# A forward FFT without butterflies until its last units, with memory handed over tile by tile, in a kernel of two joined problems

## The chip, the cores and the metric

The kernel runs on one core of one Trainium2 chip. The metric is the device time of the program in microseconds (us) on that core. The kernel before took 780.77 us, the median of three runs (777.03, 780.77 and 781.84).

TensorE (PE) multiplies matrices, VectorE (DVE), ScalarE (ACT) and GpSimd (POOL) work element by element, and SyncE (SP) issues transfers. "PEld" is the loading of PE's weights, beside PE. A transfer (DMA) is issued from a queue of SP or POOL and lands later.

## The reference, cut to what matters

Two independent problems are computed and joined along the last axis.

```python
# A: 32 heads of 18, 2048 rows in 4 segments of 512
q, k, v = x @ wq, x @ wk, x @ wv            # 2048 x 576, split into heads
M, z = 0, 0
for s in range(4):
    logits = qs @ ks.T * 18**-0.5 + mask    # causal, 512 x 512 a head
    a_dot = softmax(logits) @ vs
    a_mem = (phi(qs) @ M) / (phi(qs) @ z + 1e-6)
    o = g * a_mem + (1 - g) * a_dot         # g = sigmoid(beta)
    M, z = M + phi(ks).T @ vs, z + phi(ks).sum(rows)
a = concat(o) @ wo                          # phi(t) = t + 1 if t > 0 else exp(t)
# B: 2048 x 576
b = irfft2(rfft2(x) * (w_r + 1j * w_i), s=(2048, 576))
return concatenate([a, b], axis=-1)
```

## The kernel before, in words

float32 accuracy comes from splitting an operand into a high and a low part (a rounded copy, and what the copy leaves) and multiplying three times. The order of the instructions is written out by hand: the code runs under a manual schedule, so an engine executes its instructions in the order in which the Python code emits them. The framework adds the semaphore waits. Loops advance generators: a `yield` is a place at which another piece of work may be put in between, so moving a `yield` moves instructions in their engine's order.

There are four stages, named here by the classes `FFT` and `ATT`.

**Forward transform** (`FFT.forward`, L109 to L196, from 0 to 76.7 us). Problem B's 2048 rows are cut by 16 and transformed along both axes by matmuls, in a pipeline of 20 iterations u for 16 units. `prep` (two units ahead) forms sums and differences on DVE (`eo`, L125), their high part on ACT (`eh`, L127) and their low part on DVE (`el`, L131, and `eh`, L132). `f1` is 14 matmuls (L142). `ev0` copies the result to X on ACT (L146), and `ev1` subtracts on DVE for its low part (L149). `c1` is 12 matmuls (L162), three iterations after f1. `evz` copies c1's result from PSUM to Z on ACT (L153), four iterations after f1. The weights of the projections are loaded and split in between (`wqkl`, L391, on DVE), and the first tiles of x.

What remains of B's transform across the 16 units are radix-4 butterflies on Z: `bf` (L206; each yields after each of ten DVE instructions), `tws` (twiddles, ACT and DVE), the product with w (in `middle`) and, for the inverse, `last`. These are steps of one DVE instruction each, held in a queue, `Pace`; `take(f)` adds f to an account and runs a step for each whole unit of it. There are 266 steps in all. In the forward transform `take(1)` is called ahead of the end of prep for u below 14 (the queue has work from u = 7), and `take(2)` at the end of an iteration for u from 14.

**Projections** (`ATT.projections`, L517 on, 76.7 to 285 us). x @ wq, wk, wv in 4 segments of 13 units (`pj` and `pjv`, L445; `pm`, L502, for M and z). They run butterfly steps at an even rate that leaves `pace.left-8` as the total to be done here.

**Inverse** (`FFT.inverse`, 285 to 378 us). `ysplit` splits Z into Y (ACT, L280; the low part on POOL, L281). `i2` is 18 matmuls (L296), whose result is copied and split to T (ACT L322 and L328, DVE L324 and L329), `i3` 14 matmuls (L307), and `out` (DVE L314, L315) stores `yb` (L316). Each unit takes one butterfly step; where `ysplit(u+2)` needs a block of four that isn't finished, it runs all steps that are still missing at once (`while s.done<b and s.pace.one()`), which can be at u = 2, 6 and 10. A prologue of attention is put between: on SP's queue the loads of Qs and Ks (`stack_dmas`, L600), then the mask and beta (L840), and on PE the row maxima of the first ten heads.

**Attention** (`ATT.attention`, to the end). 133 steps t, one head each: `s1` of head t+10 gives the row maxima (L616 scores on PE, L620 and L626 on DVE; the causal block is added by a matmul of `tri` with `idb`, L625), `s2` (L660 to L670) the scores again and their exponentials on ACT, `pv` (L687) the product with v. When four heads have their maxima, `mpath` takes them to a row of Qs: `mg` on DVE and ACT, `mh` on POOL (L642 high, L643 low), a transpose on PE (`mt`, L646), a copy, and a transfer. In the loop `mpath(k+2)` is begun at hh = 1, runs its second part (mh) at hh = 2, the transpose at hh = 3, the copy right behind. `affine_select` (L672) clears what is above the diagonal, on POOL. Behind this, `run_bg` advances a list of later work: late setup (`ob`, the load of wo), `combine(g)`, which scales by reciprocals `rr` (L780 is its matmul) and adds on POOL (`am`, L786; `ol`, L776), `mem1` and `oproj`. A `lane` computes the reciprocals: for g = 1 it waits 2 more steps before loading `ux`, loading `rr` and appending combine to the list.

Memory comes from pools, which are opened and closed by stage. When a pool is closed and another takes its place, the first tile of the new one waits for everything that used the old one. So tiles of `pp` (projections) wait for all of `pf` (forward), and the tiles of attention (`tp2`, `ps`) for all of the inverse's, its stores included.

The lines on which the prediction's steps turn are these.

```python
            if t in (3,7): m=s.mpath(t//4); next(m); next(m)
...
            if hh in (2,3) and m is not None: steps(m,1)
            if hh==1 and k+2<32: m=s.mpath(k+2); next(m)
```

Of the kernel before, what the change touches and what calls it, by code (L numbers as in the profile page):

```python
# [102 lines left out]
class FFT:  # L103
# [4 lines left out]
    def forward(s,xp,cp,pp,wl,xs,consts):  # L108

        nc,io=s.nc,s.io; v=nc.vector  # L110
        xin={}; cw={}; C={}; eh={}; el={}; F={}; X={}
        def load(u):
            xin[u]=xp.tile([128,2,3,128],F32,name="xin",bufs=3)
            nc.sync.dma_start(xin[u],io["xb"][u])
        def loadc(u):
            a,b=BORD[u]
            cw[u]=cp.tile([128,2,384],F32R,name="cfw",bufs=4)
            nc.gpsimd.dma_start(cw[u],io["cfw"][4*a+b].rearrange("p (h m) -> p h m",h=2))
        def prep(u,halves=False):

            x=xin.pop(u)
            eo=xp.tile([128,2,3,128],F32,name="eo",bufs=2)
            h=xp.tile([128,2,3,128],F32R,name="eh",bufs=3)
            for r,op in enumerate((OP.add,OP.subtract)):
                v.tensor_tensor(eo[:,r],x[:,0],x[:,1],op=op)  # L125
                if halves: nc.scalar.copy(h[:,r],eo[:,r])
            if not halves: nc.scalar.copy(h,eo)  # L127
            yield
            l=xp.tile([128,2,2,128],F32R,name="el",bufs=3)
            for w in (slice(0,1),slice(1,2)) if halves else (slice(0,2),):  # L130
                v.tensor_tensor(l[:,w],eo[:,w,:2],h[:,w,:2].bitcast(F32),op=OP.subtract)  # L131
                v.tensor_tensor(h[64:97,w,2],eo[64:97,w,2],h[64:97,w,2].bitcast(F32),op=OP.subtract)  # L132
            eh[u],el[u]=h,l
            yield
        def f1(u):
            p=pp.tile([128,2,512],F32,name="f1",tag="f1")
            h,l=eh.pop(u),el.pop(u)
            for r in range(2):
                L=[(h[:,r,0],tab[:,0,r,0]),(h[:,r,1],tab[:,0,r,1]),(h[:,r,0],tab[:,1,r,0]),(h[:,r,1],tab[:,1,r,1]),
                   (l[:,r,0],tab[:,0,r,0]),(l[:,r,1],tab[:,0,r,1]),(h[:99,r,2],tab2[:99,r])]  # L140
                for n,(x,t) in enumerate(L):
                    nc.tensor.matmul(p[:,r,:FP],x,t,start=n==0,stop=n==6)  # L142
            F[u]=p
        def ev0(u):
            x=xp.tile([128,2,FP],F32R,name="X0",bufs=3); X[u]=[x]
            nc.scalar.copy(x,F[u][:,:,:FP])  # L146
        def ev1(u):
            x=xp.tile([128,2,FP],F32R,name="X1",bufs=3)
            v.tensor_tensor(x,F.pop(u)[:,:,:FP],X[u][0].bitcast(F32),op=OP.subtract)  # L149
            X[u].append(x)  # L150
        def evz(u):
            a,b=BORD[u]
            for r,p in enumerate(C.pop(u)): nc.scalar.copy(s.Z[:,b,a,r],p[:,:FP])  # L153
        def c1(u):
            a,b=BORD[u]; x=X.pop(u); cc=cw.pop(u)
            for r in range(2):
                p=pp.tile([128,512],F32,name="c1",tag="c1")
                n=0
                for (i,hl) in ((0,0),(0,1),(1,0)):
                    for q in range(2):  # L160
                        k=(0 if q==0 else 2) if r==0 else (1 if q==0 else 0)
                        nc.tensor.matmul(p[:,:FP],cc[:,hl,k*128:(k+1)*128],x[i][:,q],start=n==0,stop=n==5)  # L162
                        n+=1
                C.setdefault(u,[]).append(p)
        load(0)
        tab=cp.tile([128,2,2,2,FP],F32R,name="ftab",bufs=1)
        tab2=cp.tile([128,2,FP],F32R,name="ftab2",bufs=1)
        nc.gpsimd.dma_start(tab[:,0],io["ftab"][:,:4*FP].rearrange("p (r c f) -> p r c f",r=2,c=2))
        late=consts()
        nc.gpsimd.dma_start(tab[:,1],io["ftab"][:,4*FP:].rearrange("p (r c f) -> p r c f",r=2,c=2))  # L170
        nc.gpsimd.dma_start(tab2,io["ftab2"].rearrange("p (r f) -> p r f",r=2))
        load(1); load(2); late()
        for u in range(2): loadc(u)
        p=[prep(u,True) for u in range(2)]
        for i in range(2):
            for x in p: next(x)
        load(3)
        s.pace=Pace(61+165+40)
        for u in range(20):
            p=prep(u+2) if u+2<16 else iter(())  # L180
            if 0<u<17: ev0(u-1)
            if 3<u: evz(u-4)
            if u%4==3 and u>6: s.pace.add(s.stage1((u-7)//4))
            next(p,None)
            if 0<u<17: ev1(u-1)
            if u<14: s.pace.take(1)
            next(p,None)
            if u<16: f1(u)
            if u+4<16: load(u+4)
            elif u<18: next(xs,None)  # L190
            if 2<u<19: c1(u-3)
            if 0<u<15: loadc(u+1)
            if 1<u: next(wl,None)
            if u>13: s.pace.take(2)
        for _ in wl: pass
        for _ in xs: pass  # L196
    def bf(s,x,y,inv):
# [173 lines left out]
class ATT:  # L371
# [147 lines left out]
    def projections(s,xp,tp,pp,wv,pace,hook):  # L519

        live=[]
        s.nid=wv.tile([128,128],BF,name="nid"); s.nc.scalar.activation(s.nid,s.ident,AF.Copy,scale=-1.0)
        lw=s.load_w("wv",576,wv,xp,288,"xl",4)
        def advance():
            for l in list(live):
                try: next(l)
                except StopIteration: live.remove(l)
        tot=pace.left-8
        for g in range(4):
            if g<3: xq=[s.xprep(g+1,t,(xp,s.x0)[g%2],xp,[128,512],"xst",2) for t in range(5)]  # L530
            for i in range(13):
                u=s.qk_unit(g,i,tp,pp) if i<9 else s.v_unit(g,i-9,tp,pp)
                if i==4 and g<3: s.pk=tp.tile([128,4,576],F32,name="pk",bufs=1)
                next(u)
                hook(g,i)
                next(lw,None); next(lw,None)
                if g<3 and i in (4,6,8,10,12): next(xq[(i-4)//2])
                if g<3 and i in (1,3,5,7,9): next(xq[(i-1)//2])
                w=tot/(36+16*2.4)*(1.0 if i<9 else 2.4)
                advance()  # L540
                pace.take(w*.4)
                advance()
                next(u)
                pace.take(w*.6)
                live.append(u)
        while live: advance()

    def att_setup(s,cp):
# [1 line left out]
        s.Qs=[cp.tile([128,8,512],BF,name=f"Qs{i}") for i in range(3)]  # L550
        s.Ks=[cp.tile([128,8,512],BF,name=f"Ks{i}") for i in range(4)]
        for i in range(4): nc.gpsimd.dma_start(s.Ks[i][108:110].rearrange("p h c -> p (h c)"),io["neg1"])
        s.mask=cp.tile([128,512],F32,name="mask"); s.tri=cp.tile([128,128],BF,name="tri"); s.idb=cp.tile([128,128],BF,name="idb")
        s.bt,s.gt,s.g1=[cp.tile([128,1],F32,name=n) for n in ("bt","gt","g1")]
        d=lambda n,sh,dt: s.dp.tile(sh,dt,name=n)
        s.uD=[d(f"uD{i}",[576,512],F32) for i in range(4)]
        s.rD=[d(f"rD{i}",[32,512],F32) for i in range(4)]
# [76 lines left out]
    def mpath(s,k):  # L634
# [2 lines left out]
        mx=s.mx.pop(k); mg=s.mg.pop(k)  # L637
        nc.vector.tensor_reduce(out=mg[:,:,2:3],in_=mx[:,:,:3],axis=mybir.AxisListType.X,op=OP.max)
        nc.scalar.copy(mg[:,:,0:1],mx[:,:,3:])
        yield  # L640
        mh=s.sm.tile([128,2,16],BF,name="mh",bufs=1); mg=mg.rearrange("p h i -> p (h i)")
        nc.gpsimd.tensor_copy(mh[:,0],mg)  # L642
        nc.gpsimd.tensor_tensor(mh[:,1],mg,mh[:,0],op=OP.subtract)  # L643
# [190 lines left out]
    def prologue(s):  # L834

        nc,io=s.nc,s.io
        for i,f in enumerate(s.stack_dmas(0,0)+s.stack_dmas(0,1)):
            f()
            if i%2==1: yield
        nc.sync.dma_start(s.mask,io["mask"]); nc.sync.dma_start(s.bt,io["beta"])  # L840
        s.load_v(0)
        q=s.stack_dmas(1,0)+s.stack_dmas(1,1)+s.stack_dmas(2,1)+[lambda: s.load_v(1)]
        for i in range(2): yield
        s.masks()
        i=0
        for t in range(10):
            for _ in s.s1(t):
                if q and i%3<2: q.pop(0)()
                i+=1
                yield  # L850
            if t in (3,7): m=s.mpath(t//4); next(m); next(m)
            if t in (4,8): next(m); next(m,None)
        assert not q
    def homes(s):
# [2 lines left out]
    def attention(s,tp,ps):  # L857
# [6 lines left out]
        m=None  # L864
# [12 lines left out]
        for t in range(133):  # L877
# [8 lines left out]
            if st==10 and g>0:  # L886
                def ln(g=g):
                    r=s.recip(s.rD[g-1],s.rrD[g-1],s.g1,False,"rr")
                    for i in range(6):
                        next(r); yield  # L890
                    for i in range(2 if g==1 else 0): yield
                    for u in range(3): s.ux_load(g-1,u)
                    yield from r
                    bg.append(s.combine(g-1))
# [14 lines left out]
            steps(a,1)  # L909
            if hh==3 and m is not None: steps(m,1)  # L910
            steps(b,1)
            if hh in (2,3) and m is not None: steps(m,1)
            if hh==1 and k+2<32: m=s.mpath(k+2); next(m)
            if t>=8 and t%4==0:
                s.pv_out((t-8)//4)
# [61 lines left out]
class PP:  # L977
    def __init__(s,tc,name,bufs): s.tc,s.nm,s.bufs=tc,name,bufs
    def __enter__(s):
        s.cm=s.tc.tile_pool(name=s.nm,bufs=1,space=PSUM); s.p=s.cm.__enter__(); return s  # L980
    def __exit__(s,*a): return s.cm.__exit__(*a)
    def tile(s,sh,dt,name,tag): return s.p.tile(sh,dt,name=name,tag=tag,bufs=s.bufs[tag])
def arrays(x,wq,wk,wv,wo,beta):
# [2 lines left out]
        wo=host_wo(f(wo)).reshape(126,-1),beta=np.repeat(f(beta),4).reshape(128,1),**atables())  # L986
def emit(nc,tc,io):
    def pool(es,name,bufs=1,**kw):
        return es.enter_context(tc.tile_pool(name=name,bufs=bufs,**kw))
    with ExitStack() as L0:  # L990
        cp=pool(L0,"cp"); dp=pool(L0,"dp",space=bass.MemoryType.DRAM)
        A=ATT(nc,tc,io,cp,dp)
# [62 lines left out]
```

## Time and profile before

| | |
|---|---|
| median of three runs | 780.77 us |
| the profiled execution | 779.13 us |
| its span, first to last instruction | 777.3 us |
| PE busy | 718.0 us, 92% of the span |
| mean granted clock of PE | 0.98 |
| bytes moved | 121.64 MB, 156 GB/s |

In a line of the timeline the first number is the start in us from the span's start, the second the duration, then engine, source line, operation, the tiles written and read with their shape, and the count of instructions in the row; in brackets stands the idle time of the engine just before, and what ended it. In a row of windows stand the stretch, its length, the busy time (and count) of PE, PEld, DVE, ACT and POOL, the granted clock of PE as a share of full speed, the busy share of the DMA engines, and GB/s. In a row of groups stand line, engine, operation, tiles, count, busy time, mean ns of one, and the idle time before them. "SPq" is the issue of a transfer, at the time of its issue. What ended a wait is inferred: where several semaphores were waited for, the last by the profile is named.

### The profile page before, as it was taken

What the parts mean: (1) busy time and instruction counts of PE and PEld (TensorE: products, weight loads), DVE (VectorE), ACT (ScalarE), POOL (GpSimd) and SP (SyncE); (2) the same over time, 40 slices, a digit from 0 to 9 for tenths busy, and PEclk for the clock granted to TensorE, in tenths of its full rate; (3) what the DMA queues carried; (4) which work ended last, traced back from release to release, by engine and by line L of the source; (5) the groups of instructions that cost most, each with busy time, mean ns of one, the idle gap of its engine ahead of it and who ended that gap; (6) DMA issues with size and microseconds to landing.
All of it is one profiled execution on the core that took longest, in us unless ns stands there. A gap on an engine that the chain in (4) does not pass through costs nothing.

```text
span 777.3 us, 14564 instructions
## 1 busy us (share of the span) xinstructions
PE 718.0 (92%) x5007; PEld 498.3 (64%) x5007; DVE 546.2 (70%) x1266; ACT 467.5 (60%) x1012; POOL 212.0 (27%) x405
## 2 busy tenths in 40 slices
PE   4998999999999988499898999799999899998997
PEld 4987779788798788499643444333565335642486
DVE  6999878997898875287686878676566665573133
ACT  3666794774784735144486777676566665666621
POOL 2110000101001136154154333362224731337200
PEclk9999999999999999699999999999999999998999
DMA  9883535552642476667477656755447554340142
GB/s 321 280 245 113 174 129 188 188 187 98 225 157 93 165 251 152 171 195 198 130 157 189 168 133 139 180 148 151 119 112 196 142 152 120 91 125 26 27 142 82
DMA packets 81934, 121.64 MB, mean 156 GB/s; under 512 B 8280, under 2 KB 48742, under 8 KB 81724
## 3 DMA queue, kind: packets, MB, share of 16 engines
q1 hardware_dynamic: 75300, 104.63, 46.7%
q0 software_dynamic: 6560, 16.08, 7.3%
q8 instruction: 40, 0.66, 0.3%
q14 instruction: 34, 0.28, 0.1%
HBM read 81.97 MB, written 38.50 MB: 155 GB/s over the span
## 4 chain that ended last, share of the span: by engine, by line
PE 72%; DMA 8%; DVE 7%; ACT 5%; POOL 3%; issue 3%; SPq 0%; DVEq 0%; ACTq 0%; POOLq 0%
PE pj L445 13%; PE pv L687 9%; PE s L616 9%; PE pjv L445 7%; PE po L801 6%; PE i L307 4%; PE i L296 4%; PE s L660 3%; PE s L664 2%; PE po L830 2%; PE s L669 2%; DVE eo L125 2%; PE s L625 2%; DMA xin<-xb 2%; PE pm L502 2%
## 5 line engine op out<-in xcount | busy, mean ns | idle before, releaser
L620 DVE CUSTOM_DVE_ANT_0 junk<-s,mask 128x512 bf16<-128x512 f32 (+1 forms) x256 | 141.6, 553 | 40.5 <-PE s L616 30.4
L616 PE MATMUL s<-Ks,Qs 108*128 108x384 bf16 (+3 forms) x512 | 141.8, 306 | 15.5 <-DMA mask<-mask 11.3
L626 DVE TENSOR_REDUCE mx<-s 128x4 f32<-128x512 f32 x128 | 88.1, 688 | 58.2 <-PE s L625 53.9
L616 PEld LDWEIGHTS <-Qs 108*128 108x128 bf16 x512 | 50.1, 98 | 101.8 <-issue 88.5
L661 ACT ACTIVATE P<-s 128x512 f32<-128x512 f32 x128 | 76.8, 600 | 45.6 <-PE s L660 35.8
L672 POOL TENSOR_SCALAR_AFFINE_SELECT P<-P 128x512 f32<-128x512 f32 x128 | 76.9, 637 | 82.4 <-ACT P L661 82.3
L687 PE MATMUL pv<-P,vs 128*32 128x512 f32 (+3 forms) x1024 | 97.6, 453 | 1.1 <-issue 0.3
L670 ACT ACTIVATE P<-s 128x256 f32<-128x256 f32 x128 | 49.3, 385 | 50.7 <-PE s L669 50.3
L666 ACT ACTIVATE P<-s 128x512 f32<-128x512 f32 x128 | 76.3, 596 | 0.8 <-PE s L665 0.5
L445 PE MATMUL pj<-xh,wqkh 128*128 128x512 f32 x180 | 71.2, 395 | 0.5 <-ACT Z L153 0.5
L445 PE MATMUL pj<-xh,wqkl 128*128 128x512 f32 x180 | 71.1, 395 | 0.0
L445 PE MATMUL pj<-xl,wqkh 128*128 128x512 f32 x144 | 61.8, 429 | 0.0
L660 PE MATMUL s<-Qs,Ks 110*128 110x512 bf16 x128 | 49.3, 385 | 2.5 <-ACT P L661 1.8
L206 DVE TENSOR_TENSOR Z<-t,t 128x290 f32<-128x290 f32 (+1 forms) x96 | 48.7, 556 | 0.1
L445 PE MATMUL pjv<-wvh,xh 128*128 128x288 f32 x160 | 48.1, 303 | 0.0
L445 PE MATMUL pjv<-wvl,xh 128*128 128x288 f32 x160 | 46.2, 295 | 0.0
L206 DVE TENSOR_TENSOR t<-Z 128x580 f32<-128x580 f32 x64 | 45.7, 756 | 0.0
L625 PE MATMUL s<-tri,idb 128*128 128x128 bf16 x256 | 43.6, 222 | 0.5 <-ACT idb L566 0.5
L492 POOL MEMSET vt<- 128x32 f32 x16 | 2.3, 162 | 150.2 <-PE pm L502 125.2
L296 PE MATMUL i<-civ,Y 128*128 128x256 f32 (+1 forms) x288 | 40.6, 293 | 2.8 <-ACT Y L280 1.0
L664 PE MATMUL s<-Qs,Ks 110*128 110x384 bf16 x128 | 42.3, 331 | 0.0
L142 PE MATMUL f<-ftab,eh 128*128 128x290 f32 (+1 forms) x160 | 31.1, 313 | 10.0 <-DMA ftab<-ftab 10.0
(162 smaller groups left out, 1622.6 us busy)
## 6 DMA issues: line engine op xcount, KB each, us to landing
qkD<-sp SPq DMA_DIRECT2D x36, 384.0 KB
Qs<-qkD SPq DMA_DIRECT2D x96, 144.0 KB
Ks<-qkD SPq DMA_DIRECT2D x96, 144.0 KB
xin<-xb SPq DMA_DIRECT2D x16, 384.0 KB
cfw<-cfw POOLq DMA_DIRECT2D x16, 384.0 KB, 4.4
civ<-civ POOLq DMA_DIRECT2D x16, 384.0 KB, 4.3
vs<-vD SPq DMA_DIRECT2D x16, 330.0 KB
vD<-vt SPq DMA_DIRECT2D x16, 311.0 KB
```

The source lines that it names most:

```text
L206: v.tensor_tensor(o,a,b,op=op)
L296: nc.tensor.matmul(p[:m,k],Y[i][:,q,c*128:c*128+m],cc[:,hl,o:o+256],start=n==0,stop=n==5)
L445: s.nc.tensor.matmul(out,a,b,start=i==0,stop=i==len(L)-1)
L616: nc.tensor.matmul(out,Q[:108,h,128*i:128*i+128],K[:108,h,:128*(i+1)],start=True,stop=True)
L620: nc.vector.tensor_tensor_reduce(out=junk[:,:w],in0=src,in1=s.mask[:,512-w:],scale=1.0,scalar=-3.0e38, op0=OP.add,op1=OP.max,accum_out=s.m ...
L625: nc.tensor.matmul(pa[:,o+w-128:o+w],s.idb,s.tri,start=False,stop=True,skip_group_check=True)
L626: nc.vector.tensor_reduce(out=s.mx[k][:,hh],in_=pa.rearrange("p (b c) -> p b c",c=128),axis=mybir.AxisListType.X,op=OP.max)
L660: nc.tensor.matmul(p0,kk(0),q(0),start=True,stop=True)
L661: nc.scalar.activation(P[0][:,hh],p0,AF.Exp,scale=SC)
L666: nc.scalar.activation(P[1][:,hh],p1,AF.Exp,scale=SC)
L672: sel=lambda x,pat: nc.gpsimd.affine_select(out=x,in_=x,pattern=pat+[[1,128]],compare_op=OP.is_ge,fill=0.0,base=0,channel_multiplier=-1)
L687: nc.tensor.matmul(s.pvt[32*hh:32*hh+32,128*j:],vt[:,j,19*h:19*h+32],mv[0][:,hh,mv[1]],start=jj==0,stop=jj==3,skip_group_check=True)
```

## The change

- In the forward transform `evz(u-4)` is emitted ahead of `ev0(u-1)`, so on ACT the copies to Z stand ahead of the copy to X.
- The butterfly steps of the forward transform, one per iteration below u = 14 and two from there, become one for u = 16 to 19.
- The projections run steps up to 18 from the end (before: 8), which leaves 18 for the inverse.
- The loads of mask and beta move from the prologue, behind twelve loads of Qs and Ks, to `att_setup`, ahead of the first of them.
- In `mpath` the first `yield` goes, so mh follows mg at once; in the prologue one `next(m)` goes, and in the loop the advance at hh = 2.
- The lane of g = 1 waits 3 steps where it waited 2.
- All pools, in SBUF and PSUM, hand memory over tile by tile: a new tile waits for the users of the old tiles whose memory it overlaps, and not for the whole old pool.

```diff
@@ FFT.forward
             p=prep(u+2) if u+2<16 else iter(())
+            if 3<u: evz(u-4)
             if 0<u<17: ev0(u-1)
-            if 3<u: evz(u-4)
             if u%4==3 and u>6: s.pace.add(s.stage1((u-7)//4))
             next(p,None)
             if 0<u<17: ev1(u-1)
-            if u<14: s.pace.take(1)
             next(p,None)
             if u<16: f1(u)
...
             if 1<u: next(wl,None)
-            if u>13: s.pace.take(2)
+            if u>15: s.pace.take(1)
@@ ATT.projections
-        tot=pace.left-8
+        tot=pace.left-18
@@ ATT.att_setup
-        s.mask=cp.tile([128,512],F32,name="mask"); s.tri=cp.tile([128,128],BF,name="tri"); s.idb=cp.tile([128,128],BF,name="idb")
+        s.mask=cp.tile([128,512],F32,name="mask"); nc.sync.dma_start(s.mask,io["mask"]); s.tri=cp.tile([128,128],BF,name="tri"); s.idb=cp.tile([128,128],BF,name="idb")
         s.bt,s.gt,s.g1=[cp.tile([128,1],F32,name=n) for n in ("bt","gt","g1")]
+        nc.sync.dma_start(s.bt,io["beta"])
@@ ATT.mpath
         nc.scalar.copy(mg[:,:,0:1],mx[:,:,3:])
-        yield
         mh=s.sm.tile([128,2,16],BF,name="mh",bufs=1); mg=mg.rearrange("p h i -> p (h i)")
@@ ATT.prologue
-        nc.sync.dma_start(s.mask,io["mask"]); nc.sync.dma_start(s.bt,io["beta"])
         s.load_v(0)
...
-            if t in (3,7): m=s.mpath(t//4); next(m); next(m)
+            if t in (3,7): m=s.mpath(t//4); next(m)
@@ ATT.attention
-                    for i in range(2 if g==1 else 0): yield
+                    for i in range(3 if g==1 else 0): yield
...
-            if hh in (2,3) and m is not None: steps(m,1)
+            if hh==3 and m is not None: steps(m,1)
@@ PP.__enter__
-        s.cm=s.tc.tile_pool(name=s.nm,bufs=1,space=PSUM); s.p=s.cm.__enter__(); return s
+        s.cm=s.tc.tile_pool(name=s.nm,bufs=1,space=PSUM,reuse_waits="tile"); s.p=s.cm.__enter__(); return s
@@ emit
-        return es.enter_context(tc.tile_pool(name=name,bufs=bufs,**kw))
+        return es.enter_context(tc.tile_pool(name=name,bufs=bufs,reuse_waits="tile",**kw))
```

## The prediction

> **What bounds the kernel now.** I read the page's first part, then its chain of work, then the busy time by windows, then the timeline of each place where the chain leaves PE.
>
> ```profile
> span 777.3 us, 14564 instructions
> PE 718.0 (92%) x5007; PEld 498.3 (64%) x5007; DVE 546.2 (70%) x1266; ACT 467.5 (60%) x1012; POOL 212.0 (27%) x405
> PE 72%; DMA 8%; DVE 7%; ACT 5%; POOL 3%; issue 3%; SPq 0%; DVEq 0%; ACTq 0%; POOLq 0%
> ```
>
> PE is the bound, and what an edit is worth is the PE idle time that it takes away, plus what that idle time does to PE's clock. By windows (length, busy time of PE, PEld, DVE, ACT, POOL, granted clock, DMA share, GB/s):
>
> ```profile
> 27.23:34.89 7.66, 7.66 (x57) 7.42 (x56) 6.96 (x13) 5.11 (x10) 1.06 (x2) 1.00 0.93 282
> 43.14:51.40 8.26, 7.58 (x54) 7.10 (x53) 8.13 (x16) 5.11 (x10) 1.06 (x2) 1.00 0.87 264
> 76.67:284.94 208.27, 206.52 (x1168) 174.84 (x1168) 180.61 (x338) 140.11 (x275) 13.69 (x63) 1.00 0.51 171
> 321.65:371.50 49.85, 49.85 (x381) 46.76 (x379) 37.64 (x94) 19.98 (x49) 19.87 (x29) 0.96 0.63 173
> ```
>
> The first two rows are two forward units each, without and with butterflies: 7.66 against 8.26 us, and in the second DVE is full (8.13 of 8.26). The third is the projections, PE full; the fourth the inverse after its stall, PE full. So DVE sets the pace in the forward transform alone, which the change relieves, and has 27.7 us free in the projections (208.27 - 180.61) and 12.2 in the inverse, where it puts the work.
>
> **Forward transform.** Before, seven units of u=7 to 13 carry one butterfly step each, and u=14 to 19 two each: 19 steps. After, u=16 to 19 carry one each: 4. PE's first c1 rows of two units, and DVE's rows between its eo's, one eo per unit:
>
> ```profile
> 27.28 1.78 PE L162 MATMUL c<-X,cfw 128*128 128x290 f32 x12
> 30.80 1.78 PE L162 MATMUL c<-X,cfw 128*128 128x290 f32 x12
> ...
> 31.06 1.02 DVE L125 TENSOR_TENSOR eo<-xin 128x384 f32<-128x384 f32 x2
> 33.04 0.69 DVE L131 TENSOR_TENSOR el<-eo,eh 128x512 fp32r<-128x512 f32 x1 [0.29 <-ACT eh L127]
> 34.89 1.02 DVE L125 TENSOR_TENSOR eo<-xin 128x384 f32<-128x384 f32 x2
> 47.27 1.02 DVE L125 TENSOR_TENSOR eo<-xin 128x384 f32<-128x384 f32 x2
> 48.88 0.75 DVE L206 TENSOR_TENSOR t<-Z 128x580 f32<-128x580 f32 x1
> 51.40 0.55 DVE L125 TENSOR_TENSOR eo<-xin 128x384 f32<-128x384 f32 x1
> ```
>
> A unit lasts 34.89 - 31.06 = 3.83 us without a step and 51.40 - 47.27 = 4.13 with one: a step of 0.75 costs 0.30, because it fills the 0.29 in which DVE otherwise waits for ACT's eh. Seven units give -2.1 us. The eight steps taken from u=14 to 19 stand behind the last units' ACT and PE chain, and I count them at nothing. The copies to Z now precede the X copy on ACT:
>
> ```profile
> 46.56 1.89 PE L162 MATMUL c<-X,cfw 128*128 128x290 f32 x12 [0.35 <-ACT Z L153]
> 70.08 3.48 PE L162 MATMUL c<-X,cfw 128*128 128x290 f32 x24 [0.77 <-ACT Z L153]
> 76.67 0.50 PE L445 MATMUL pj<-xh,wqkh 128*128 128x512 f32 x1 [0.49 <-ACT Z L153]
> ```
>
> In full units PE's 0.35 is hidden by DVE; in the last ones, where PE leads, X's copy stands ahead of the Z for which c1 waits: -0.3 of the 0.77. The first projection waits 0.49 for the last Z copy only because all of the forward's PSUM is handed over as one; its own bank has long been read: -0.5. Sum -2.9; bounds -0.5 (only that last wait goes) and -4.8 (the seven units fall to PE's own 30.80 - 27.28 = 3.52, so 7 x 0.61, and the wait goes too).
>
> **Projections.** 244 steps instead of 239 under the same PE work: 5 x 0.6 = 3 us of DVE against 27.7 free: 0. If that cover were gone, +3.
>
> **Inverse.** DVE finds 19 steps instead of 9. The first take their places one per unit; the rest come as bursts where ysplit(8) and ysplit(12) need them, ahead of that unit's T1 subtraction: two full-width and four half-width steps.
>
> ```profile
> L206 DVE TENSOR_TENSOR Z<-t,t 128x290 f32<-128x290 f32 x12 | 4.7, 459 | 0.0
> 326.67 0.75 DVE L206 TENSOR_TENSOR Z<-t,t 128x580 f32<-128x580 f32 x1
> 327.98 0.69 DVE L324 TENSOR_TENSOR T<-i,T 128x512 fp32r<-128x512 f32 x1 [0.56 <-ACT T L322]
> 330.53 0.64 PE L296 MATMUL i<-civ,Y 128*128 128x256 f32 x4
> ```
>
> At u=6, 326.67 becomes the 0.75 that stands there and five steps more with their successor's first (some 3.0), so T1 ends near 331.1 instead of 328.67 (327.98 + 0.69); i2 of the next unit, which needs its PSUM buffer, starts at 330.53: +0.6. ACT's T copy of 99 rows queues behind the Y copies that wait for the burst, with like slack. At u=10 the burst replaces 0.83 us of steps already there and ends just in time: 0. Sum +0.6; bounds 0 and +6.1 (both bursts bare).
>
> **Mask.** The page names the mask for the longest stall:
>
> ```profile
> 304.38 3.63 SPq L600 DMA_DIRECT2D Ks<-qkD  x4
> 309.40 0.36 SPq L840 DMA_DIRECT2D mask<-mask  x1
> 320.46 0.48 PE L616 MATMUL s<-Ks,Qs 108*128 108x384 bf16 x1 [11.28 <-DMA mask<-mask]
> 320.84 0.30 ACT L565 CAST tri<-mask 128x128 bf16<-128x128 f32 x1 [10.57 <-DMA mask<-mask]
> 321.39 0.29 PE L625 MATMUL s<-tri,idb 128*128 128x128 bf16 x1 [0.45 <-ACT idb L566]
> ```
>
> But L616 reads Qs and Ks, not the mask, and it started 0.38 before ACT's copy of the mask could. The mask was issued behind the last Ks piece on the same queue, so what ended PE's wait was Ks. Moved ahead of rD it passes all twelve Qs and Ks loads, which still wait behind the inverse's stores of yb as now. It costs SP one issue (0.36) before the first Qs, which are early. Gone is what follows: L625 comes 0.93 after L616, and needs 0.3: -0.6; bounds 0 and -11.3.
>
> **Attention's start.** The first exponential waits for memory of the whole inverse:
>
> ```profile
> 378.95 0.38 PE L660 MATMUL s<-Qs,Ks 110*128 110x512 bf16 x1 [0.66 <-PE s L625]
> 381.50 0.60 ACT L661 ACTIVATE P<-s 128x512 f32<-128x512 f32 x1 [4.31 <-DMA yb<-yout]
> 382.15 0.38 PE L660 MATMUL s<-Qs,Ks 110*128 110x512 bf16 x1 [1.83 <-ACT P L661]
> 411.19 0.48 PE L616 MATMUL s<-Ks,Qs 108*128 108x384 bf16 x1 [2.42 <-DMA ob<-wo]
> ```
>
> As built, it then waits for its scores and for loads long landed, so it can start at 379.4, and the ob load behind the same yb with it. PE's 1.83 goes: -1.8; bounds 0 (the loads at 411.19 are late by as much more) and -2.2.
>
> **The maximum's path in attention.** mh moves one step earlier in POOL's order; where nothing is in front of it (most k) that is worth 0. At two places combine's additions are:
>
> ```profile
> 611.74 0.23 PE L646 MATMUL mt<-idb,mh 128*32 128x128 bf16 x1 [1.37 <-POOL mh L643]
> 708.09 1.25 POOL L786 TENSOR_TENSOR am<-ux,am 72x512 f32<-72x512 f32 x1
> 709.30 0.19 POOL L642 CAST mh<-mg 128x16 bf16<-128x16 f32 x1
> 709.84 0.23 PE L646 MATMUL mt<-idb,mh 128*32 128x128 bf16 x1 [2.75 <-POOL mh L643]
> ...
> 411.21:414.62 3.41, 3.41 (x16) 1.05 (x16) 1.39 (x3) 1.19 (x2) 0.48 (x3) 0.50 0.63 142
> 711.58:718.41 6.83, 6.10 (x17) 1.38 (x16) 0.69 (x1) 3.53 (x8) 3.62 (x6) 0.50 0.02 5
> ```
>
> In the built order mh overtakes two of these POOL operations at the last place (2 x 1.23 = 2.5 of 2.75) and more at the first: -1.4 and -2.5. The selects still end before pv needs them. After 2.75 us idle PE ran 6.83 us at half clock; its 6.10 us of matmuls would take 3.05 at full clock, and I take 2.5 back, since some of them also wait for ACT. Bounds for all three: 0 and -7.5 (1.37 + 2.75 + 3.4).
>
> PE also ran at half clock right behind the gap of 2.42 at 411.19 (the 411.21 row), so gaps of this size go with it. [...]
>
> **The later combine.** For g=1, ux, rr and all of combine come a step later.
>
> ```profile
> 502.99 0.49 PE L780 MATMUL pb<-rr,sel 64*126 64x512 f32 x1 [3.77 <-DMA rr<-rrD]
> 503.37:506.78 3.41, 3.41 (x17) 1.11 (x16) 2.08 (x4) 1.20 (x2) 0.00 (x0) 0.50 0.74 165
> ```
>
> On SP, two more Qs and Ks loads pass ahead of rr, which then lands about as much later as PE asks later: 0; bounds -5.5 (gap and half clock gone, 3.77 + 1.7) and +2.2 (a step).
>
> **Sum.** -2.9 + 0 + 0.6 - 0.6 - 1.8 - 1.4 - 2.5 - 2.5 + 0 = -11.1 on the profiled execution's own 779.13 (span 777.3): 768.0. The median of the runs shown, 780.77, is 1.6 above that execution.
>
> **Rivals.** (a) The gains are given back inside attention: the loads at 411.19 take the 1.8, and PE's gap at 709.84 only moves, to the selects behind the same POOL operations, so 2.5 + 2.5 go as well: 768.0 + 6.8 = 774.8. For it: DMA is at 0.63 behind that gap (411.21); against it: the selects keep their places. Chance 0.27, with the half-way cases, the forward's gain missed among them.
> (b) PE really waits for the mask. Then Ks lands some 4 to 8 us before 320.46, and the sum is 6 us better: 762. For it stands the page's attribution, against it the 0.38. Chance 0.08.
> (c) Slower: the bursts uncover PE in the inverse. T1, ACT's Y and T copies and POOL's low parts chain behind them; each burst is then 3.0 of idle PE, and if that lowers the clock as the mask stall does,
>
> ```profile
> 309.00:326.00 17.00, 5.27 (x24) 4.48 (x23) 2.58 (x6) 2.14 (x7) 2.27 (x3) 0.60 0.74 186
> ```
>
> so by 17 x 0.4 = 6.8, the price is 2 x (3.0 + 6.8) = 19.6: 787. It decides from some 2.4 us of idle, the shortest gap above that had half clock behind it; I reckon with 0.6 and 0. Chance 0.08.
> (d) The hand-over by tile doesn't do what it says, since every first tile overlaps something late: -0.5 and -1.8 go, 770.3. Against it are the waits as built. Chance 0.05.
> (e) The half clock after 709.84 has another cause than the gap, and stays: 770.5. Against it is the 411.21 row. Chance 0.05.
>
> **How the numbers follow.** My forecast has the other 0.47: 768.0, with its own range 764 to 773 from the forward's bounds and the combine's. The range for 8 in 10 is 761 to 777: it takes in (b), (d), (e) and (a), and leaves out (c). About 1% is what a measurement of this kernel tells from no change, 7.8 us, so the border is 773 beside 780.8. Faster: 0.47 x 0.9 + (b) 0.08 + (d) 0.04 + (e) 0.04 + a fifth of (a) = 0.64. Slower: about (c)'s 0.08, though its 787 needs little more to pass 788.6. The same: 0.28.
>
> **What would show it.** Right: eo rows 3.83 apart to u=13 and the first pj near 73.8; PE's wait at the first L616 of the inverse still some 11 us, now with Ks named, and L625 0.3 behind it; T1 of u=6 3 us later with PE's next i2 moved by under 1; the first exponential 0.5 behind its score; PE's gap at 709.84 under 0.5 and no half clock after. Wrong: an inverse (321.65 to 371.50 now) longer by more than 2 us, a gap over 5 us at rr, or a stall of under 8 us where the mask was.

## The result, and the profile after

The changed kernel takes 791.16 us, median of six executions (783.02 to 800.76), beside 781.31 for the kernel before. The ratio is 1.0118, with a 95% interval of 1.0082 to 1.0155: 1.2% slower, where 768.0 was forecast. One of the six executions lay above the others and is left out of the ratio. The profiled execution took 792.36 us.

The page of the changed kernel, its first part and its chain of work:

```profile
span 789.6 us, 14545 instructions
PE 724.4 (92%) x5007; PEld 500.2 (63%) x5007; DVE 549.4 (70%) x1266; ACT 467.3 (59%) x1012; POOL 213.1 (27%) x405
PE 66%; DMA 10%; ACT 9%; DVE 6%; POOL 4%; issue 3%; SPq 1%; ACTq 0%; DVEq 0%; POOLq 0%
```

The span is 12.3 us longer. PE is busy 6.4 us more with the same 5007 matmuls, so part of the time went by at a lower clock (the mean granted clock is 0.974, before 0.980); and the chain now runs over ACT for 9% where it had 5. Both traces hold every matmul, so each can be laid beside its counterpart. How far the changed kernel is ahead (-) or behind (+) at the borders of the stages, in us:

| at | difference | gained or lost since the row above |
|---|---|---|
| first projections | -3.6 | -3.6 |
| end of the projections | -0.4 | +3.2 |
| end of the inverse | +3.1 | +3.4 |
| after attention's start | +1.4 | -1.6 |
| before the gap at rr | +3.3 | +1.9 |
| steps behind combine of g=1 | +10.8 | +7.4 |
| last maximum of attention (t = 117 or so) | +15.9 | +5.1 |
| end | +12.7 | -3.2 |

Places of gain and loss on PE, in the timeline of the changed kernel (its line numbers are mostly one lower than before, and the same for L616 to L626):

```profile
73.18 0.40 PE L444 MATMUL pj<-xh,wqkh 128*128 128x512 f32 x1
...
115.55 0.38 PE L469 MATMUL pj<-sp,nid 128*128 128x512 bf16 x1 [1.86 <-ACT sp L467]
...
321.53 0.48 PE L616 MATMUL s<-Ks,Qs 108*128 108x384 bf16 x1 [10.95 <-DMA vs<-vD]
321.80 0.31 PE L625 MATMUL s<-tri,idb 128*128 128x128 bf16 x1
...
332.22 1.68 PE L295 MATMUL i<-civ,Y 128*128 128x256 f32 x12 [1.66 <-DVE T L323]
...
381.19 0.38 PE L659 MATMUL s<-Qs,Ks 110*128 110x512 bf16 x1
...
393.57 0.32 PE L616 MATMUL s<-Ks,Qs 108*128 108x384 bf16 x1 [1.17 <-DMA Qs<-qkD]
...
509.69 0.79 PE L779 MATMUL pb<-rr,sel 64*126 64x512 f32 x1 [4.69 <-DMA Ks<-qkD]
...
723.30 0.23 PE L645 MATMUL mt<-idb,mh 128*32 128x128 bf16 x1 [0.31 <-POOL mh L642]
...
728.59 0.49 PE L757 MATMUL pb<-rd,sel 64*126 64x512 f32 x1 [2.08 <-ACT am L753]
```

The first projection starts at 73.18 instead of 76.67 and without a wait. The stall of 11 us at the first L616 is about as long as it was; that matmul reads Ks and Qs, although the profile names the load of v here (in after_again, below, it names Ks). The first L625 stands 0.27 behind L616 instead of 0.93. The first exponential of attention,

```profile
381.60 0.60 ACT L660 ACTIVATE P<-s 128x512 f32<-128x512 f32 x1 [1.35 <-PE s L659]
```

waits for its score alone. The transpose that waited 2.75 for mh waits 0.31. So most of the forecast's gains are there. The losses stand in between: a wait for sp in the projections, one for T in the inverse, and what happens from rr on. In windows of the changed kernel (length, busy time of PE, PEld, DVE, ACT, POOL, clock, DMA share, GB/s):

```profile
505.00:509.30 4.30, 0.00 (x0) 0.00 (x0) 0.44 (x3) 0.47 (x2) 0.41 (x2) 1.00 0.61 167
509.30:529.80 20.50, 19.33 (x80) 6.78 (x81) 10.62 (x24) 8.32 (x17) 6.83 (x8) 0.50 0.57 135
529.80:533.20 3.40, 3.40 (x35) 1.58 (x33) 2.84 (x10) 3.12 (x8) 1.98 (x4) 1.00 0.00 0
```

Behind the gap at rr PE runs for 20.5 us at half clock, busy for 19.33 of them, where before it took 3.4 us to come back.

### The profile page after: what moved, and what is told of

Its sections match the earlier page's. It is cut to its first block, busy times and chain, and to the rows that moved or that the text cites. A ratio compares the mean times of both kernels' runs of the same rounds, so it can differ in the third digit from the quotient of the medians.

```text
span 789.6 us, 14545 instructions
## 1 busy us (share of the span) xinstructions
PE 724.4 (92%) x5007; PEld 500.2 (63%) x5007; DVE 549.4 (70%) x1266; ACT 467.3 (59%) x1012; POOL 213.1 (27%) x405
## 4 chain that ended last, share of the span: by engine, by line
PE 66%; DMA 10%; ACT 9%; DVE 6%; POOL 4%; issue 3%; SPq 1%; ACTq 0%; DVEq 0%; POOLq 0%
PE pj L444 12%; PE pv L686 9%; PE s L616 8%; PE pjv L444 6%; PE po L800 5%; PE i L295 3%; DMA Qs<-qkD 3%; PE i L306 3%; PE s L659 3%; PE s L663 2%; PE po L829 2%; PE s L668 2%; PE pn L751 2%; PE pm L501 2%; DMA Ks<-qkD 2%
## 5 line engine op out<-in xcount | busy, mean ns | idle before, releaser
L616 PE MATMUL s<-Ks,Qs 108*128 108x384 bf16 (+3 forms) x512 | 144.0, 310 | 17.6 <-DMA vs<-vD 11.0
L626 DVE TENSOR_REDUCE mx<-s 128x4 f32<-128x512 f32 x128 | 88.2, 689 | 68.9 <-PE s L625 64.1
L616 PEld LDWEIGHTS <-Qs 108*128 108x128 bf16 x512 | 50.6, 99 | 104.5 <-issue 91.7
L625 PE MATMUL s<-tri,idb 128*128 128x128 bf16 x256 | 44.3, 224 | 0.0
L295 PEld LDWEIGHTS i<-civ,Y 128*128 128x128 f32 (+1 forms) x288 | 38.3, 193 | 8.0 <-DVE T L323 4.5
```

What stands on the lines that cost most here:

```text
L295: nc.tensor.matmul(p[:m,k],Y[i][:,q,c*128:c*128+m],cc[:,hl,o:o+256],start=n==0,stop=n==5)
L616: nc.tensor.matmul(out,Q[:108,h,128*i:128*i+128],K[:108,h,:128*(i+1)],start=True,stop=True)
L626: nc.vector.tensor_reduce(out=s.mx[k][:,hh],in_=pa.rearrange("p (b c) -> p b c",c=128),axis=mybir.AxisListType.X,op=OP.max)
```

## The experiments

Two theories stood against each other at first. L: the third step of the lane of g=1 is the loss, by a later combine and a long half clock. B: the butterflies moved out of the forward transform are the loss, in the projections and in the inverse. For every kernel the table gives the median time, the ratio to the kernel before with its interval, the median of PE's mean clock, and the median of span times mean clock. The last counts PE's time at half clock by half, and varies less: its standard deviation over the 23 executions of the kernel before is 1.4 us, that of the time 3.0. The kernels were run in four sets, each with the kernel before beside it: for that kernel it was 761.8, 761.8, 762.1 and 763.0 (the last beside dense and lane2_evz), so 1.2 us between kernels of different sets tell nothing by themselves.

| kernel | executions | median us | ratio, 95% interval | clock | span x clock |
|---|---|---|---|---|---|
| before (beside the first four) | 23 | 781.47 | | 0.977 | 761.8 |
| changed | 6 | 791.16 | 1.0118 (1.0082 to 1.0155) | 0.974 | 767.4 |
| after_again | 6 | 792.16 | 1.0112 (1.006 to 1.0165) | 0.9705 | 767.2 |
| lane2 | 12 | 779.81 | 0.9973 (0.9941 to 1.0005) | 0.978 | 760.9 |
| fwd_undone | 12 | 783.34 | 1.0016 (0.9989 to 1.0043) | 0.9785 | 765.3 |
| mpath_undone | 6 | 793.3 | 1.0142 (1.01 to 1.0184) | 0.970 | 766.9 |
| lane4 | 12 | 781.28 | 1.0025 (1.0 to 1.005) | 0.977 | 762.3 |
| lane2_tot8 | 12 | 778.3 | 0.9966 (0.9938 to 0.9993) | 0.977 | 759.0 |
| lane2_whole | 12 | 782.84 | 1.0022 (1.0003 to 1.0041) | 0.9775 | 762.7 |
| before_lane3 | 8 | 786.42 | 1.0073 (1.004 to 1.0105) | 0.977 | 767.0 |
| rr_ahead_odd | 12 | 785.15 | 1.0063 (1.0031 to 1.0095) | 0.9785 | 765.7 |
| rr_ahead | 12 | 780.77 | 0.9955 (0.9916 to 0.9994) | 0.9705 | 757.4 |
| lane2_mpath_undone | 12 | 781.22 | 1.0017 (0.9988 to 1.0046) | 0.977 | 762.2 |
| lane2_fwd_undone | 9 | 774.53 | 0.9926 (0.9894 to 0.9958) | 0.978 | 757.3 |
| dense | 6 | 792.36 | 1.0129 (1.0086 to 1.0173) | 0.977 | 771.2 |
| lane2_evz | 6 | 772.3 | 0.9882 (0.9847 to 0.9917) | 0.9815 | 755.6 |

**The changed kernel itself (after_again).**

> The changed kernel itself, unedited, as the measure for the other runs. Theory L (a long stretch of half clock behind the later combine): in the changed profile PE stood 4.69 us at rr and then ran 20.5 us at half clock, where before it ran 3.4; that is (20.5 - 3.4) / 2 = 8.5 us of the 12.3 us by which the two spans differ, and it should be there again: half clock of 14 us or more behind the gap at rr, about 791 us. Theory B (the butterflies moved into projections and inverse cost it): the half clock is chance, and a run without it is still 3 to 5 us above before, some 784.

Its profile came out at 783.89 us, with half clock behind the same gap for only 6.8 us (windows of this kernel):

```profile
501.00:504.70 3.70, 0.01 (x1) 0.00 (x0) 0.45 (x3) 0.47 (x2) 0.41 (x2) 1.00 0.61 164
504.70:511.50 6.80, 4.91 (x20) 1.70 (x20) 2.37 (x5) 1.27 (x3) 0.00 (x0) 0.50 0.73 176
511.50:514.90 3.40, 2.89 (x21) 1.30 (x21) 2.94 (x9) 2.29 (x6) 1.61 (x3) 0.99 0.48 145
```

So the long stretch differs from one execution to the next of the same program (20.5 and 6.8 us), which theory L did not expect. The twelve executions of both labels go from 783 us at a clock of 0.98 to 801 at 0.962; span times clock stays near 767, and that is 5.4 above before in any case.

**The lane with two steps (lane2).**

```diff
-                    for i in range(3 if g==1 else 0): yield
+                    for i in range(2 if g==1 else 0): yield
```

> The changed kernel with the reciprocals of g=1 waiting 2 steps instead of 3. Theory L: PE asks for rr a step earlier, the long half clock is the consequence of where combine's matmuls lie, and with the old place it is one window of 3.4 us again: 8 to 10 us faster than the changed kernel, 781 to 783. Theory B: within 2 us of the changed kernel, 789 to 793.

779.81: 12 us less, 6.4 of them in span times clock. Theory L's time is nearly right, its reason is not: the gap at rr is 4.91 here too, and half clock behind it lasted 6.8. The two traces run side by side through rr and then part slowly, by 0.75 us at a time, between 545 and 700 us. What differs there is how the later work falls on the steps. The loop runs 1.2 pieces a step, so two in every fifth. A tile of `oproj` has two pieces: eight matmuls, then seven and ACT's copy out of the one PSUM bank. Shifted by one step, each such pair holds the end of one tile and the start of the next. PE in after_again:

```profile
576.56 0.83 PE L800 MATMUL po<-woh,ol 126*128 126x288 f32 x5
577.88 0.94 PE L800 MATMUL po<-woh,oh 126*128 126x288 f32 x5 [0.49 <-ACT ob L802]
```

and the same pair with two steps in the lane, where the tile begins and ends within the step:

```profile
582.19 0.92 PE L800 MATMUL po<-woh,oh 126*128 126x288 f32 x5
582.94 0.83 PE L800 MATMUL po<-wol,oh 126*128 126x288 f32 x5
583.61 0.83 PE L800 MATMUL po<-woh,ol 126*128 126x288 f32 x5
```

The groups by shape, from 508 to 702 us of after_again (busy time, mean ns, idle before):

```profile
L800 PE MATMUL po<-woh,oh 126*128 126x288 f32 x64 | 12.6, 318 | 2.9 <-ACT ob L802 2.9
L751 PE MATMUL pn<-pq,Mst 126*126 126x512 f32 x16 | 8.4, 604 | 1.6 <-DVE am L758 1.6
L751 PE MATMUL pn<-pq,Mst 72*72 72x512 f32 x4 | 2.2, 621 | 1.6 <-DVE am L758 1.6
```

and from 512 to 705 us with two steps:

```profile
L800 PE MATMUL po<-woh,oh 126*128 126x288 f32 x64 | 12.5, 317 | 0.0
L757 PE MATMUL pb<-rd,sel 64*126 64x512 f32 x8 | 3.9, 490 | 1.5 <-ACT am L753 1.5
L757 PE MATMUL pb<-rd,sel 64*72 64x512 f32 x2 | 0.9, 450 | 1.4 <-ACT am L753 1.4
```

Six waits for ACT's copy, 2.9 us, appear. Each costs more than its 0.49: in the pair above the next five matmuls start 1.32 us behind the five before them, and 0.67 within a tile. The wait within `mem1` changes its place and little else (3.2 for 2.9). This is theory P, pairing. Its rival, R, says that a later combine costs by being later.

**P against R (lane4 and before_lane3).** The same line with 4 steps; and the kernel before with nothing but 3 steps.

> The changed kernel with the lane of g=1 waiting 4 steps instead of 3. Theory P (pairing): every fifth step of attention runs two pieces of the later work; with 3 the pairs are the end of one product tile and the start of the next, which must wait for ACT's copy of the only PSUM bank (45 such neighbours in the order built, 39 with 2 and 39 with 4). So 4 is like 2 again: 780 to 783, and span times clock near 761 instead of 767. Theory R (the later combine itself costs, since everything behind it is late): 4 is as slow as 3 or slower, 791 or above, span times clock 767 to 770.

> The kernel before with nothing changed but the lane of g=1, from 2 steps to 3. Theory P: the pairs of the later work fall badly here too (45 neighbours instead of 39): span times clock 5 to 7 us above before (761.8), and half clock more often behind the gap at rr; 789 to 794. Theory R: 1 to 3 us slower, 782 to 784. If the loss needs the other edits (mh earlier, or memory by tile), it is the same as before: 780 to 783.

The same group with four steps (512 to 705 us of lane4), and in the kernel before with three (500 to 705 us of before_lane3):

```profile
L800 PE MATMUL po<-woh,oh 126*128 126x288 f32 x64 | 12.4, 316 | 0.0
L801 PE MATMUL po<-woh,oh 126*128 126x288 f32 x64 | 12.6, 318 | 2.9 <-ACT ob L803 2.9
```

Four steps give 762.3 in span times clock, 1.4 above two, where R expected 767 to 770; three give 767.0 even in the kernel before. The six waits stand in all seven traces with three steps ahead of combine, and in none of the nine others. R is out as the cause of the 5 us: a shift by one step costs 5 to 6, and one by two steps 1.4, little more than the kernel before moves between the sets. What was not tried is a second PSUM bank for these tiles with the order unchanged. In time, 786.42 is less than P's 789 to 794, because the clock stayed at 0.977.

**The moved butterflies (fwd_undone, lane2_fwd_undone, lane2_tot8, lane2_evz).** The first takes the forward's order and steps and the projections' share back to before; the second does so with two steps in the lane:

```diff
-            if 3<u: evz(u-4)
             if 0<u<17: ev0(u-1)
+            if 3<u: evz(u-4)
...
+            if u<14: s.pace.take(1)
...
-            if u>15: s.pace.take(1)
+            if u>13: s.pace.take(2)
...
-        tot=pace.left-18
+        tot=pace.left-8
```

> The changed kernel with the forward transform's order of copies, its steps and the projections' share of them as before. Theory B: forward +3.6 (it had become that much shorter), projections -3.2 (PE's waits for sp go), inverse -3.3 (the bursts go, T's waits of 1.66 and 1.02 with them): 3 us faster than the changed kernel, 788. Theory L: the same 3, and 8 more or less only if the clock behind rr happens to change; half clock there is still long.

> The changed kernel with the lane at 2 steps and the forward transform and the steps' shares as before. The forward is 3.6 longer, the projections 3.2 and the inverse 3.3 shorter by the trace: 2 to 3 us faster than with the lane at 2 alone (779.8), 777, and so no better than leaving only the bursts out (778.3). If moving the steps off the forward was worth what was forecast (-2.9 + 0.6), it is 2 us slower, 782.

lane2_tot8 has only the last of these edits, and two steps in the lane; lane2_evz has all but the first, so that the copies to Z stay ahead.

> The changed kernel with the lane at 2 steps, and the projections running all but 8 of the butterfly steps (as before) instead of all but 18. Theory B (bursts): the inverse has no bursts, so PE's waits of 1.66 and 1.02 for T go, and the 10 steps more are hidden in the projections: 2.5 to 3.5 us faster than the kernel with the lane at 2 alone (779.8), about 777. A rival: DVE in the projections is late already (PE waited 1.6 and 1.5 us there for sp), and 10 steps more cost what the bursts did: 779 to 781.

> The changed kernel with the lane at 2 steps and the butterfly steps of forward and projections as before, but the copies to Z ahead of the copy to X. The forecast's term for that order is -0.3 behind the last units: 774.3 against 774.5 with the old order. A rival: ev1 on DVE waits for the X copy, which now stands behind two copies to Z (1 us), in units where DVE sets the pace: up to 13 units x 0.3 = 4 us slower, 778.

Moving the steps costs more than it brings. With two steps in the lane, span times clock goes from 760.9 to 759.0 when only the bursts are taken out, and to 755.6 with the steps back in the forward and the copies to Z ahead: 5.3 us in all, 7.5 by the time. lane2_tot8's 778.3 lies between what its two theories expect: the waits for T of 1.66 and 1.02 are gone, but the projections, with ten steps more, last 214.2 us in its trace, where they last 211 to 212 with 18 left and 208 in the kernel before. lane2_fwd_undone gained 5, twice what was expected. The order of the copies by itself gives 1.7 (757.3 to 755.6; 774.53 to 772.3 by the time), which is not clear of the noise; in the two traces the stretch from the eo near 27 us to the first projection falls from 48.76 to 47.60, so 1.2 of it are there, more than the 0.3 forecast, and the rival with 4 us more is out. The last kernel is 1.2% faster than the kernel before. fwd_undone came out 8 to 9 us below the changed kernel where 3 were expected; 2 of these stand in span times clock, the rest is the clock.

Where the steps hurt, in the changed kernel: DVE in the inverse (the second row is the last of the first row's six steps; the third is POOL's),

```profile
326.61 3.91 DVE L205 TENSOR_TENSOR Z<-t,t 128x580 f32<-128x580 f32 x6
329.07 1.45 DVE L205 TENSOR_TENSOR Z<-t,t 128x290 f32<-128x290 f32 x1
328.84 2.11 POOL L280 TENSOR_TENSOR Y<-Z,Y 128x512 fp32r<-128x512 f32 x2 [15.02 <-ACT Y L279]
330.44 1.13 DVE L205 TENSOR_TENSOR t<-Z 128x580 f32<-128x580 f32 x1
331.49 0.68 DVE L323 TENSOR_TENSOR T<-i,T 128x512 fp32r<-128x512 f32 x1
```

and ACT in the projections:

```profile
110.44 0.70 ACT L215 ACTIVATE tw<-Z 128x580 f32<-128x580 f32 x1
...
113.34 0.67 ACT L216 ACTIVATE tw<-Z 128x580 f32<-128x580 f32 x1
113.92 0.60 ACT L415 CAST xh<-xst 128x512 fp32r<-128x512 f32 x1
114.43 0.58 ACT L480 COPY pk<-ptr 128x512 f32<-128x512 f32 x1
114.90 0.59 ACT L467 CAST sp<-pj 128x512 bf16<-128x512 f32 x1
```

The burst is seven steps and 4.9 us (326.61 to 331.49), not 3.0 to 3.7, and PE waits 1.66 behind it. Two of its steps run beside POOL's subtractions for the low part of Y and take 1.45 and 1.13 us, where such steps away from them take 0.45 and 0.75: 1.4 more together. The second burst has the same (1.46 at 350.01 and 0.83 at 351.39). In lane4 and mpath_undone only one step of the first burst is lengthened, by 1.0, and PE's wait behind it is 0.74 and 0.88. In the projections six twiddle products, 3.5 us of ACT in a row, stand ahead of the sp for which PE waits 1.86. Half clock can follow too: in four of the eleven traces that have the moved steps (after_again, lane2, lane2_tot8, rr_ahead) a stretch of it of 3.4 or 6.8 us stands behind the wait for sp near 97 us, of 1.45 to 2.39; in none of the five with the steps as before does it.

**The maximum's path and the hand-over (mpath_undone, lane2_mpath_undone, lane2_whole).** The first two put the `yield` in mpath and the two advances back, with 3 and with 2 steps in the lane; the third takes `reuse_waits="tile"` from all pools.

> The changed kernel with mh as before, one step later than mg. The row of the maxima comes later again, so the gaps that it ended (1.37 and 2.75 us and half clock behind the second) come back: 4 to 7 us slower than the changed kernel, 795 to 798, if mh's place was worth what the trace shows (-1.3 at the first, -3.2 at the second). A rival: mh in front of POOL's other work delays ol and am and so feeds the wait at rr; then undoing it gives 1 to 3 us back instead.

> The changed kernel with the lane at 2 steps and mh one step later again, as before. By the prediction's terms the gaps of 1.4 and 2.75 come back, and some 2.5 for the clock behind the second: 4 to 6.5 us slower than with the lane at 2 alone (779.8), 784 to 786; by the trace of that kernel (-1.4 and -3.1 at the two places) 4.5. Rival: ACT's am and POOL's ol end these stretches anyway and only the first comes back: 781.

> The changed kernel with the lane at 2 steps and every pool handed over as a whole, as before. By the prediction's terms the forward's last wait (0.5) and the first exponential's (1.8) come back: 2.3 us slower than the kernel with the lane at 2 alone, 782. Rival: what the earlier start of attention gains is taken back by the Qs and Ks loads (1.4 and 1.0 us of waits there that were not in before), so nothing changes: 779 to 781.

With two steps mh's new place gives 1.4 us by the medians (779.81 to 781.22, 1.3 in span times clock), which is not clear of the noise, and with three nothing that shows. In the traces its gaps come back when it is undone, as 1.34 and 2.75 with two steps and as 0.61 and 1.30 with three. The hand-over by tile is worth 1.8 in span times clock, 3.0 by the time, near the 2.3 forecast; in the trace of lane2_whole both waits are back (0.49 and 1.76).

**The gap at rr (rr_ahead_odd, rr_ahead).** Both have 2 steps before the loads of ux and rr and more behind them: one, so that PE's order is that of the changed kernel, or two, together with lane2_tot8's share of steps.

```diff
-                    for i in range(3 if g==1 else 0): yield
+                    for i in range(2 if g==1 else 0): yield
...
                     yield from r
+                    for i in range(1 if g==1 else 0): yield
```

> The changed kernel with PE's order left as it is, but the loads of ux and rr one step earlier: the lane of g=1 waits 2 steps before them and 1 behind them. Theory P with G (the gap at rr sets off the half clock that differs from run to run): the bad pairs stay, so span times clock stays 4 to 6 us above the kernel with the lane at 2; the gap of 4.7 falls to 2 or 3 us and the clock's mean rises from 0.9725 to 0.978 or more: 783 to 787. If the clock was lost to the bad pairs and not to the gap, the time stays at 790 to 793 with a clock of 0.97.

> The changed kernel without bursts (8 steps left for the inverse), with the loads of ux and rr at the place of a wait of 2 steps and combine 2 steps behind them, so that the pairs are good and PE asks for rr some 4 to 5 us later. Theory G: against the kernel that has the same without the 2 steps behind (778.3) the gap of 4.7 at rr shrinks below 1, and its half clock goes: 4 to 7 us faster, 771 to 774. Rival: PE idles the same elsewhere, since what waited behind the gap (Qs and Ks loads) is late by itself: 777 to 779.

With PE's order unchanged and rr one step earlier the gap falls to 1.82, the clock's median rises from 0.9725 (twelve executions of the changed kernel) to 0.9785, and the time falls by 6 to 785.15, while span times clock stays at 765.7: the pairs stay bad, the clock is better. That is as expected, but it doesn't show that the length of the gap sets the clock: in lane2 and before_lane3 the gap is 4.91 and the clock's median 0.978 and 0.977. In rr_ahead the rival was right about the place, with a time of 780.77 for its 777 to 779: PE no longer waits for rr, but 3.60 us at a matmul that reads Qs and Ks (the profile names the load of uD, which stands among theirs on SP's queue), and half clock follows for 17 us all the same:

```profile
502.30:505.80 3.50, 0.00 (x0) 0.00 (x0) 0.39 (x3) 0.46 (x2) 0.41 (x2) 1.00 0.63 137
506.90:524.00 17.10, 16.32 (x71) 5.37 (x69) 9.08 (x22) 7.28 (x15) 5.61 (x7) 0.50 0.61 149
```

Its twelve executions fall apart: five at a clock of 0.98 or more take 771 to 777 us, seven at 0.967 to 0.972 take 780 to 788.

**Denser matmuls behind the gap (dense).** Two score matmuls of s1 are executed twice in ten steps, to see whether the stretch of half clock behind rr gets shorter.

```diff
+        if 62<=t<72: mm(pa[:,0:384],2)
...
+        if 62<=t<72: mm(pc,3)
         mm(pc,3); red(pc,3)
```

> The changed kernel with two score matmuls of s1 (384 and 512 columns, 128 x 128 of bf16) executed twice in attention steps 52 to 61, where PE ran at half clock for 20.5 us: work that changes no result and costs about 0.4 us a step at full clock, 4 us in all. [...] Rival (the stretch is chance, whatever runs): the mean clock stays at 0.97 and the time goes to 795 or more.

Half clock lasted 10.2 us in the profile, where the two profiles of the changed kernel have 20.5 and 6.8; the clock's median is 0.977 and the time 792.36, where the rival has 0.97 and 795 or more. Over six executions this settles nothing.

## Why the prediction was wrong, point by point

Two steps failed. The larger is "The later combine": "0; bounds -5.5 and +2.2 (a step)". It priced the lane's third step by what PE waits for rr, and named nothing behind combine. But the list of later work advances at a fixed rate of pieces, and this shift by one step turned the double steps from one whole tile into two halves. It cost 6.4 us in span times clock (lane2), 5.2 in the kernel before (before_lane3), and 12 by the medians of the changed kernel, whose clock is lower too. In the traces the six waits for ob account for 2.9 of it, and for some 4 with the later start of the matmuls behind them; a wait for rr of g=2, which only the seven kernels with this shift have, for 0.4 to 2.1, and the waits in mem1 for 0.3.

The other is the moved steps, "Projections" and "Inverse": put at 0 and +0.6, they cost 3.2 and 3.4, and 5.3 in span times clock net of what the forward gains by losing them.

- **Forward transform: -2.9.** Near in size, -3.6, but in part by compensation. The units' eo rows stand 3.83 apart up to 50.38 us; five intervals fell from 4.12 to that, which is 1.5 and not 2.1. Another 2.2 came behind the last eo (from 60.51 to 76.67 before, from 59.20 to 73.18 after), where 0.8 was forecast; the copies' order has about 1.2 of it, not 0.3.
- **Projections: 0, +3 "if that cover were gone".** Wrong, +3.2, about the bound given. The cover was counted on DVE, which had 27.7 us free; by the waits that the profile names the price arose in ACT's order, where twiddles stand together ahead of sp.
- **Inverse: +0.6.** Wrong, +3.4 in all. The path was right: PE's next i2 starts at 332.22, as T's subtraction ends (331.49 + 0.68). The size was not: the subtraction came 3.5 us later than before (331.49 beside 327.98), where the working has 2.4, and PE waited 1.66 there and 1.02 at the second burst, which was put at 0. The 1.4 us by which steps beside POOL's work are lengthened in each burst was in no term; without it, by an estimate from these rows, the waits would be 0.3 and 0, near the forecast. Some 0.8 more stands at the start of the inverse, where PE waits 1.46 for POOL's low part of Y at 288.04, and 0.65 before. Rival (c) named the bursts, with 3.0 and a half clock behind each; behind these no half clock came in this profile, but in rr_ahead_odd's 3.4 us of it lie at 332.4.
- **Mask: -0.6.** Right: 0.66 less between the rows of L616 and L625, and a stall of 11 us stays (10.95 beside 11.28), so rival (b) is out.
- **Attention's start: -1.8.** Right in place (-1.6), and rival (a) in part: 1.9 is given back up to rr, in waits of 1.17 at 393.57 (0.46 before) and of 1.39 at 433.15 (none before); the one near 411, which (a) named, is 2.04 beside 2.42.
- **mh: -1.4 and -2.5, and -2.5 for the clock.** The gaps went, but the medians show 1.4 at most. At the second place the wait moved: 2.08 for am at 728.59 stands where PE had waited 0.73. This wait is 1.05 to 2.1 in every kernel with mh in its new place, with two, three or four steps in the lane. The half clock of 6.83 behind the old gap is gone in the changed kernel's profile; in those of after_again, lane4 and lane2_evz 3.4 of it follow the wait for am.
- **The clock.** The half clock behind the gap at rr was taken as the same before and after. Its median over the executions fell from 0.977 to 0.9725, about 4 us; rr_ahead_odd, with the same order on PE and a smaller gap, has it back. Why lane2 keeps 0.978 with a gap as long isn't shown.

Together: span times clock rose by 5.4, which is 6.4 for the pairs and 5.3 for the moved steps, less 6 or 7 for copies, mask, hand-over and mh (755.6 in lane2_evz, which has these alone, beside 761.8 to 763.0). The clock adds the other 4 or 5. What stays open is why the same program takes 7 or 20 us to come back to full clock.

## What to carry to other kernels

Where work is advanced at a fractional rate, the pieces that meet in one step depend on where the list starts; after shifting it, look at which pieces share a PSUM bank back to back (six waits, 2.9 us here), and try a shift by one step and by two. An engine's free time in a stage doesn't make a moved step free: its helpers (ACT's twiddles here) and its place in each queue count, and a forced burst came whole ahead of T's subtraction here (4.9 us of DVE, 1.4 of them in steps that took longer beside POOL's subtractions; PE waited 1.66). One edit of a bundle can hide the gains of the others: taken apart, this change held a kernel that is 1.2% faster.

## What the runs showed of the hardware that was not expected

Behind the gap at rr (4.69 us) PE stayed at half clock (0.50) for 20.5 us while it was busy for 19.33 of them (80 matmuls, 33 of them with 32 columns and 5 with 64 rows), and in another execution of the same program came back after 6.8, busy for 4.91 of them (the 504.70 row of after_again). In rr_ahead_odd a gap of 1.82 us, and one of 0.40 behind it, were followed by a stretch at half clock two microseconds later (windows of that kernel):

```profile
505.90:507.80 1.90, 0.08 (x2) 0.03 (x1) 0.50 (x3) 0.47 (x2) 0.41 (x2) 1.00 0.63 182
509.90:513.30 3.40, 3.40 (x16) 1.05 (x13) 1.83 (x7) 1.01 (x3) 0.00 (x0) 0.50 0.73 211
```

In the changed kernel DVE's butterfly steps and POOL's subtractions took longer where they ran at the same time. The half-width steps that start outside POOL's subtractions take at most 0.46 us; of the four that start within one, two take 1.45 and 1.46, the others 0.51 and 0.83. The other way round, POOL's first four subtractions of the inverse take 4.45 us with a DVE step among them (286.20), and 3.62 before, where that step (285.73, 0.76 long) ends 0.12 behind their start. DVE's subtraction for T takes 0.68 to 0.69 us in every unit, the one at 335.75, which starts within one of POOL's, too. No run takes POOL's part away, so that the one lengthens the other is read from the overlap alone.
